# The output stores issued from GpSimd, one transfer of 122 rows in place of 112 + 10 from SP

## Chip, cores, metric

One core of a Trainium2 chip. The metric is the device time of one execution in microseconds (us), on this one core. A time is the median of all runs of a kernel in its call. A run over 1.5% above the fastest of its kernel counts as slow, and ratios use the fast runs alone. "One look" is a single run, whose state is unknown. The profiled execution's span is a little shorter than its time (229.1 us in an execution timed at 230.8).

## The reference

x has shape (8, 3264, 192). A causal convolution over the sequence, seven taps, softmaxed per head, gives a new x. Its first 64 Fourier modes are mixed by complex matrices w_r and w_i, and the result is added back:

```python
X = np.fft.rfft(x, axis=1)                    # x: output of the 7-tap convolution
Yr = einsum(Xr, w_r) - einsum(Xi, w_i)        # modes 0..63
Yi = einsum(Xr, w_i) + einsum(Xi, w_r)
y = np.fft.irfft(Y, n=S, axis=1)
u = x + y
return u + np.maximum(u @ w_ch, 0.0)          # (8, 3264, 192), float32: 20.05 MB
```

What matters here is the output: 8 * 3264 = 26112 rows of 192 floats, 768 bytes each.

## The kernel before

The sequence is cut into 27 windows of 122 rows (the last has 92). A window lies on 122 partitions, so that six rows of history fit beside it in the 128. The loads, which also cast to bf16, go from GpSimd (POOL), all but one small one. The last stage makes two windows of two batches at a time, adds them on VectorE (DVE) into a tile t of four windows, and stores:

```python
p3 = ctx.enter_context(tc.tile_pool(name="p3", bufs=4, side="right"))     # the t tiles
...
def store(q, w0, nw, t):                    # nw = 4 windows, 2 at the end of a pair of batches
    for i in range(2):                      # the two batches of a tile
        dst = out[2 * q + i, WIN * w0:WIN * (w0 + nw), :].rearrange("(k p) e -> p k e", p=WIN)
        for r0, r1 in ((0, 112), (112, WIN)):
            nc.sync.dma_start(out=dst[r0:r1], in_=t[r0:r1, 0:nw, D * i:D * i + D])
...
def finish(item):
    ...
    group_y(combos, zp, t, 2 * k)           # two matmuls, then the add on DVE that writes t (L425)
    if k + 1 == len(work[n]):
        if w0 == NWIN - 1:                  # twice: the 92-row windows of four batches
            dst = out[2 * q:2 * q + 4, WIN * w0:S, :].rearrange("b p e -> p b e")
            nc.sync.dma_start(out=dst, in_=t[0:LASTVALID, 0:2, :].rearrange("p k (b e) -> p (k b) e", b=2))
        else:
            store(q, w0, 2 * len(work[n]), t)
```

There are 56 calls of the inner loop over batches (48 with four windows, 8 with two), so 112 transfers, and two transfers of 92 rows.

Of the kernel before, what the change touches and what calls it, by code (L numbers as in the profile page):

```python
# [18 lines left out]
def kernel(  # L19
# [9 lines left out]
    nc = tc.nc  # L29
    B, S, D = x.shape  # L30
# [6 lines left out]
    WIN = 122  # L37
# [122 lines left out]
    for half in range(2):  # L160
        hs = slice(4 * half, 4 * half + 4)
        for k in range(KK):
            nc.vector.copy_predicated(  # L163
                out=cband[:, hs, :],
# [178 lines left out]
    for g in range(NG4):  # L343
# [20 lines left out]
        for t in range(2):  # L364
            nc.tensor.transpose(et[:, t, :], ymix[:, 64 * t:64 * t + P], ident[:])
        nc.vector.tensor_copy(out=yeT[:, :, 4 * g:4 * g + 4, :],
                              in_=et[:, :, :].rearrange("p t (q k) -> p t q k", q=4)[:, :, :, 0:16])
# [59 lines left out]
    def store(q, w0, nw, t):  # L427
        for i in range(2):
            dst = out[2 * q + i, WIN * w0:WIN * (w0 + nw), :].rearrange("(k p) e -> p k e", p=WIN)
            for r0, r1 in ((0, 112), (112, WIN)):  # L430
                nc.sync.dma_start(out=dst[r0:r1], in_=t[r0:r1, 0:nw, D * i:D * i + D])  # L431

    work = []
    for q in range(B // 2):
# [8 lines left out]
    def finish(item):  # L443
        (n, k, combos), zp = item
        if k == 0:
            tcur[n] = p3.tile([P, 4, 2 * D], F32, tag="t", name="t")
        t = tcur[n]
        group_y(combos, zp, t, 2 * k)
        if k + 1 == len(work[n]):
            q, w0 = work[n][0][0]  # L450
            if w0 == NWIN - 1:
                dst = out[2 * q:2 * q + 4, WIN * w0:S, :].rearrange("b p e -> p b e")
                nc.sync.dma_start(out=dst,
                                  in_=t[0:LASTVALID, 0:2, :].rearrange("p k (b e) -> p (k b) e", b=2))
            else:
                store(q, w0, 2 * len(work[n]), t)
# [47 lines left out]
```

## Time and profile before

| | before |
|---|---|
| time, median | 229.21 us |
| store stage | from about 138 us to the end |
| stores at the 16 DMA engines | busy for 0.92 of their time (the DMA share), about 250 GB/s |
| DVE waiting for a store to free a t buffer | 7.1 us, 8 times |

The kernel has stages with different limits. Only the last one has stores, so it is read by itself: the views restricted to a window, not the averages over the span. The prediction below shows its lines.

### The profile page before, as it was taken

How to read it: one execution, taken by the hardware profiler on the slowest of the kernel's cores; microseconds unless marked ns; L12 is line 12 of the kernel's file. 1: busy time of each engine (PE TensorE's matmuls, PEld its weight loads, DVE VectorE, ACT ScalarE, POOL GpSimd, SP SyncE). 2: the span in 40 equal slices, each digit the busy share in tenths (PEclk: the TensorE clock that was granted, in tenths of full speed). 3: DMA queues.
4: the chain of work that ended last, by engine and by line, in shares of the span. 5: the costliest groups of instructions: out<-in, count | busy, mean ns of one | idle time of the engine just before them, and what ended most of it. 6: DMA issues, size and time to landing. Idle time of an engine off the chain costs nothing.

```text
span 229.1 us, 4342 instructions
## 1 busy us (share of the span) xinstructions
PE 167.1 (73%) x1699; PEld 131.8 (58%) x1699; DVE 116.4 (51%) x211; ACT 101.4 (44%) x132; POOL 70.6 (31%) x121
## 2 busy tenths in 40 slices
PE   0037349989988786768869679999899899989300
PEld 0014248777877564547647458778677677767200
DVE  7897001111111577776654615677676566666510
ACT  2017978778687010100431126566556456546200
POOL 8996343443290457574856000000000000000000
PEclk9999999999999689997995979999999999999965
DMA  2999999999998389999999401899899789988992
GB/s 28 180 177 192 192 192 192 192 192 193 184 140 142 54 129 141 156 163 140 145 183 159 83 1 38 232 245 253 217 269 254 214 207 263 249 250 241 263 263 61
DMA packets 65340, 40.50 MB, mean 177 GB/s; under 512 B 31016, under 2 KB 65320, under 8 KB 65320
## 3 DMA queue, kind: packets, MB, share of 16 engines
q0 software_dynamic: 37600, 20.14, 67.4%
q1 hardware_dynamic: 27720, 20.09, 31.8%
q8 instruction: 13, 0.21, 0.4%
q14 instruction: 7, 0.06, 0.1%
HBM read 40.31 MB, written 20.05 MB: 263 GB/s over the span
## 4 chain that ended last, share of the span: by engine, by line
DMA 33%; PE 31%; DVE 14%; POOL 8%; issue 3%; ACT 3%; SPq 3%; DVEq 0%; POOLq 0%; ACTq 0%
DMA x_all<-in_x_dram 16%; DMA out_dram<-t 8%; DVE cT L273 6%; PE tp L271 6%; DMA wt<-in_moe_w_i_dram 6%; DVE t L425 5%; PE zp L400 5%; PE zp L407 5%; PE zp L405 5%; POOL x_all L63 5%; PE zp L414 4%; DMA win<-in_moe_w_ch_dram 4%; SPq L431 3%; ACT x_all L233 2%; PE yp L349 2%
## 5 line engine op out<-in xcount | busy, mean ns | idle before, releaser
L425 DVE TENSOR_TENSOR t<-zp,x_all 122x768 f32<-122x768 f32 (+1 forms) x54 | 51.3, 957 | 32.3 <-PE zp L414 21.7
L409 ACT ACTIVATE zp<-zp 128x768 f32<-128x768 f32 x54 | 42.9, 795 | 31.4 <-PE zp L407 31.4
L233 ACT CAST x_all<-cp 122x960 bf16<-122x960 f32 (+2 forms) x48 | 39.5, 884 | 22.5 <-PE cp L227 22.3
L405 PE MATMUL zp<-win,cT 128*128 128x192 bf16 x216 | 45.2, 249 | 0.0
L227 PE MATMUL cp<-x_all,cband 128*128 128x240 bf16 (+2 forms) x192 | 27.7, 286 | 19.7 <-DVE cband L163 15.2
L400 PE MATMUL zp<-zwi,gst 128*128 128x384 bf16 x108 | 35.9, 332 | 5.4 <-DVE t L425 4.0
L273 DVE COPY cT<-tp 128x854 bf16<-128x854 bf16 (+2 forms) x48 | 26.9, 590 | 18.3 <-PE tp L271 17.8
L227 PEld LDWEIGHTS <-cband 128*128 128x128 bf16 x192 | 19.4, 108 | 25.2 <-DVE cband L163 15.6
L63 POOL DMA_DIRECT2D x_all<-in_x_dram x24 | 23.8, 1001 | 15.9 <-DMA x_all<-in_x_dram 15.9
L271 PE MATMUL tp<-ident,tl 122*128 122x122 bf16 x112 | 23.2, 243 | 7.0 <-DVE tl L240 5.4
L211 POOL DMA_DIRECT2D wt<-in_moe_w_r_dram x32 | 19.3, 602 | 28.3 <-PE yp L349 21.7
L271 PE MATMUL tp<-ident,x_all 122*128 122x122 bf16 x216 | 26.4, 242 | 2.1 <-DVE cT L273 1.9
L284 PE MATMUL xp<-x_all,fst 122*128 122x192 bf16 (+1 forms) x216 | 22.3, 252 | 7.4 <-ACT fst L178 6.2
L405 PEld LDWEIGHTS <-cT 128*128 128x128 bf16 x216 | 21.4, 99 | 10.5 <-issue 7.7
L414 PE MATMUL zp<-zwi,gst 128*128 128x384 bf16 x108 | 26.2, 326 | 0.2 <-ACT zp L409 0.2
L407 PEld LDWEIGHTS <-cT 128*128 128x128 bf16 x216 | 21.4, 99 | 7.4 <-issue 0.5
L357 ACT CAST ymix<-yp 128x192 bf16<-128x192 f32 x16 | 5.1, 319 | 44.2 <-PE yp L349 44.2
L284 PEld LDWEIGHTS <-fst 122*128 122x128 bf16 (+1 forms) x216 | 18.4, 100 | 8.8 <-ACT fst L178 6.6
L407 PE MATMUL zp<-win,cT 128*128 128x192 bf16 x112 | 23.3, 248 | 0.0
L271 PEld LDWEIGHTS <-x_all 122*128 122x128 bf16 x216 | 18.9, 110 | 5.7 <-issue 4.8
L407 PE MATMUL zp<-wB,cT 128*128 128x192 bf16 x104 | 21.9, 251 | 0.0
L288 DVE CAST xs<-xp 128x192 bf16<-128x192 f32 x8 | 2.9, 358 | 34.3 <-PE xp L284 34.3
(76 smaller groups left out, 158.9 us busy)
## 6 DMA issues: line engine op xcount, KB each, us to landing
out_dram<-t SPq DMA_DIRECT2D x48, 336.0 KB
wt<-in_moe_w_r_dram POOLq DMA_DIRECT2D x32, 144.0 KB, 5.1
wt<-in_moe_w_i_dram POOLq DMA_DIRECT2D x32, 144.0 KB, 5.1
x_all<-in_x_dram POOLq DMA_DIRECT2D x8, 432.0 KB, 16.1
x_all<-in_x_dram POOLq DMA_DIRECT2D x9, 384.0 KB, 17.7
x_all<-in_x_dram POOLq DMA_DIRECT2D x7, 480.0 KB, 18.4
out_dram<-t SPq DMA_DIRECT2D x48, 30.0 KB
out_dram<-t SPq DMA_DIRECT2D x8, 168.0 KB
```

The source lines that it names most:

```text
L63: nc.gpsimd.dma_start(out=x_all[:, b, c0:c0 + n, :], in_=src)
L227: nc.tensor.matmul(cp[:, j, 0:GRP * n].rearrange("p (w e) -> p w e", w=n), cband[:, h, :], x_all[:, b, w0:w0 + n, GRP * h:GRP * h + GRP], ...
L233: nc.scalar.copy(out=dst, in_=srcv)
L271: nc.tensor.transpose(tp[:, WIN * k:WIN * k + WIN], slot_lhsT(b, u, tl, a + k), ident[0:WIN, 0:WIN])
L273: nc.vector.tensor_copy(out=cT[:, b, WIN * a:WIN * (a + cnt)], in_=tp[:, 0:WIN * cnt])
L284: nc.tensor.matmul(xp[:, 0:D], fst[0:k, c, :], x_all[0:k, b, c, :], start=(c == 0), stop=(c == NWIN - 1))
L400: nc.tensor.matmul(zp[:, k, 0:2 * D], gst[:, WIN * w:WIN * w + P], zwi[:, 2 * q:2 * q + 2, 0, :], start=True, stop=False, skip_group_check ...
L405: nc.tensor.matmul(o, cT[:, b, WIN * sa:WIN * sa + P], win0[:, 0:D], start=False, stop=False, skip_group_check=True)
L407: nc.tensor.matmul(o, cT[:, b, WIN * sb:WIN * sb + P], wBs[par], start=False, stop=(i == 1), skip_group_check=True)
L409: nc.scalar.activation(out=zp[:, :, 0:2 * D], in_=zp[:, :, 0:2 * D], func=ACT.Relu)
L414: nc.tensor.matmul(zp[:, k, 0:2 * D], gst[:, WIN * w:WIN * w + P], zwi[:, 2 * q:2 * q + 2, 1, :], start=False, stop=True, skip_group_check ...
L425: nc.vector.tensor_tensor(out=tv, in0=yv, in1=xv, op=ALU.add)
```

## The change

The intent is to take the issue of the stores off SP, to halve their number, and to give the queue of GpSimd, idle by then, something to do.

```diff
     def store(q, w0, nw, t):
         for i in range(2):
             dst = out[2 * q + i, WIN * w0:WIN * (w0 + nw), :].rearrange("(k p) e -> p k e", p=WIN)
-            for r0, r1 in ((0, 112), (112, WIN)):
-                nc.sync.dma_start(out=dst[r0:r1], in_=t[r0:r1, 0:nw, D * i:D * i + D])
+            nc.gpsimd.dma_start(out=dst, in_=t[0:WIN, 0:nw, D * i:D * i + D])
```

The two 92-row transfers stay on SP.

## The prediction

> **What bounds the kernel now.** I read the page first, its 40 slices of busy time, to find the stages:
>
> ```profile
> PE   0037349989988786768869679999899899989300
> DVE  7897001111111577776654615677676566666510
> POOL 8996343443290457574856000000000000000000
> DMA  2999999999998389999999401899899789988992
> GB/s 28 180 177 192 192 192 192 192 192 193 184 140 142 54 129 141 156 163 140 145 183 159 83 1 38 232 245 253 217 269 254 214 207 263 249 250 241 263 263 61
> q1 hardware_dynamic: 27720, 20.09, 31.8%
> ```
>
> A slice is 5.73 us. From slice 24 (about 138 us) on the kernel only stores, PE is near full, and POOL, whose queue carried all loads, is empty. The 20.05 MB output leaves here at about 250 GB/s, so the changed transfers are all in this last stage. Next, the table of stretches cuts it finer (columns after the stretch: its length, then PE, weight loads, DVE, ACT, POOL, the clock, the DMA share, GB/s):
>
> ```profile
> 150.00:160.00 10.00, 10.00 (x94) 8.00 (x93) 7.20 (x9) 5.95 (x8) 0.00 (x0) 1.00 0.92 250
> 180.00:190.00 10.00, 9.26 (x83) 7.24 (x81) 6.20 (x8) 5.35 (x7) 0.00 (x0) 1.00 0.78 205
> 210.00:220.00 10.00, 4.04 (x34) 2.71 (x31) 5.13 (x6) 2.38 (x3) 0.00 (x0) 0.95 0.92 257
> 220.00:229.00 9.00, 0.00 (x0) 0.00 (x0) 0.00 (x0) 0.00 (x0) 0.00 (x0) 0.50 0.47 135
> ```
>
> The reader is to see that the DMA engines stay at 0.92 while PE has already gone quiet, and that nothing but DMA runs in the last 9 us. Then the waits of the stretch from 131 us, and the chain of work that ended last, near its end:
>
> ```profile
> DVE t L425 <- PE zp L414: 21.7, 38, 5.7
> DVE t L425 <- DMA out_dram<-t: 7.1, 8, 1.8
> ```
> ```profile
> 207.66 0.33 PE zp L414 x2
> ...
> 210.72 0.97 DVE t L425
> 211.71 0.96 SPq L431
> 212.71 0.46 SPq L431
> 213.22 4.16 DMA out_dram<-t
> 217.60 0.95 DVE t L425
> ```
>
> DVE's adds into t wait 8 times, 7.1 us in all, for a store to give a t buffer back, and the chain runs through such stores: the stage is bound by the stores, with PE close behind. PE's own pace is 1.31 us per pair of windows (such pairs of L414 rows follow each other at 165.07, 166.38 and 167.69 in the chain), so 54 pairs need 70.7 us; from the first zp at 134.1 to PE's end at 214.3 it took 80.2. Last, the timeline of the SP queue:
>
> ```profile
> 213.22 9.18 SPq L431 DMA_DIRECT2D out_dram<-t  x14
> 222.50 0.26 SPq L453 DMA_DIRECT2D out_dram<-t  x1
> ```
>
> The final t is ready at 218.55, but its store (92 rows, L453) is not issued before 222.50, as SP still works through earlier issues. Then it moves alone; the span ends at 229.1.
>
> **How the stores are spread now.** Queue 1 counts 27720 packets. 8*3264 = 26112 are pieces of 768 bytes of the output, 128 are rows of wraw, and 1480 remain. If 112 rows post a count on 16 engines, 10 rows on 10, 92 rows on 4 and wraw on 16, that is 56*(16+10) + 2*4 + 16 = 1480, exactly. So in a pair of transfers ten engines carry 4*(7+1) = 32 pieces and six 28: mean 30.5, or 0.953 of the most loaded, which is the 0.92 to 0.95 that the share shows when full. The time of a piece is 0.318*16*229.1/27720 = 42 ns per packet, 44 ns when the small ones (about 9 ns each in the packet records) are taken out. The four engines that also carry L453 hold 26*8*8 + 2*92 = 1848 pieces, so 1848*44 ns = 81.3 us, of the 85 us between the first issue at 141.4 plus 1.2 and the end. In the final L453 alone the packet records show one piece per 33 ns per engine.
>
> **What the Trainium skill says.** (1) "DMA: Bandwidth & Descriptors", section "Why a DMA increments its semaphore by 16 and not by 1": the number of engines is the largest up to 16 that divides the slowest dimension. That makes 112 rows 16, 92 rows 4, 122 rows only 2; the packet count above agrees for SP. It adds that transfers issued from GpSimd get, for "some direct copies", all 16 engines with the row count over 16 rounded up per engine. The trace before can't confirm this: its GpSimd transfers have 128, 112, 96, 64, 10 or 2 rows. (2) Same page, "Issuing engines are not separate DMA queues": another issuer saves issue time only. The trace agrees that issue is worth something at the end (3.95 us between 218.55 and 222.50). (3) Same page, "Why small descriptors are slow (HBM only)": bytes/32 beats plus about 3 cycles, so 27 cycles for 768 bytes; at the page's 850 MHz an estimated 31.8 ns. The 33 ns of the lone L453 agrees; the 44 ns of the bulk is a third above it, a backlog that appears only when many engines write. (4) Same page, "Latency and other measured facts": first byte 1 us after a GpSimd issue, 0.6 us after a hardware one. The trace has GpSimd's first small loads landing in 2.0 to 2.5 us.
>
> **The change, part by part.**
> Removed: 112 issues on SP (median 0.53 us, 60 us of SP's time). Only the two of L453 remain there (the instruction order shows it), so the last one can go right after its add: at most 3.95 us gained at the end.
> Added: 56 issues on POOL. From the page's rows,
>
> ```profile
> L63 POOL DMA_DIRECT2D x_all<-in_x_dram x24 | 23.8, 1001 | 15.9 <-DMA x_all<-in_x_dram 15.9
> L211 POOL DMA_DIRECT2D wt<-in_moe_w_i_dram x32 | 19.6, 612 | 1.9 <-DMA x_all<-in_x_dram 1.4 <-issue 0.5
> ```
>
> 612 ns for 128 pieces and about 1000 for some 1150, hence about 0.38 ns a piece: 612 + 360*0.38 = 0.75 us for the 488 pieces of a store, 48*0.75 + 8*0.66 = 41 us in all, on an engine with no work from 138 us on. Against the SP path a store starts about 0.5 us later, its twin 0.75 us after it.
> Waits: the instruction order has each store wait for the one 8 transfers earlier on its kind of queue. On SP that was two t tiles (4 transfers each); from GpSimd it is four tiles, just as many as there are t buffers. So dips in feeding, like 0.78 at 180 to 190 us, should shrink.
> Moved bytes: the same. With 8 rows an engine (rounded up from 122/16) fifteen engines carry 32 pieces and one 8: the most loaded engine has 32 as before. No gain from balance.
> Sum, if all 16 engines are used: at 44 ns a piece the four worst engines need 81.3 us from about 143.1, so 224.4, plus 1.2 us to the end as now, 225.6. At 40 ns a tile takes 64*40 = 2.56 us, below PE's 2.62: PE binds. The first L414 at 138.65 plus 53*1.31 plus three more zwi groups of about 0.6 gives 210, plus 1 for the add, 0.6 for issue, 1 for the start, 92*40 ns = 3.7 of L453, which shares its four engines with the last backlog (2 more), plus 1.2: 219.5. I expect between these, near 222, as queue 0 kept a steady 192 GB/s into bf16 from twice as many source bytes for 40 us, so that descriptors written by GpSimd do not by themselves slow an engine at 768 bytes.
>
> **Rivals.**
> A: 122 rows get only 2 engines each. A store takes 244 pieces, at 33 to 44 ns 8.1 to 10.7 us. A tile's buffer is held 2.3 (fill) + 1.5 (two issues) + 1 + about 9.4 = 14.2 us; four buffers give a tile per 3.55 us against 2.62 of PE. 24 full tiles and 4 halves at some 2.2 make 94 us, then a tail of 10: about 246. For it: the divisor rule, which SP obeys to the packet, and the before kernel's own split of GpSimd loads into 112 + 10 and 96 + 2. Against it: the page's exception. I give it 0.3.
> B: all engines, but stores are slower by this path, say 50 ns a piece (descriptors are fetched from SBUF, and rows are now 8*768 bytes apart between engines): 143.1 + 1848*0.050 + 1.2 = 236.7. Nothing in the trace speaks for it, as no store goes this way yet; 0.15.
> C: the bulk is limited by what HBM takes, 265 GB/s whoever issues. Then only feeding and the tail improve: 224 to 228, about the same. That the lone L453 ran at 33 ns and the bulk at 44 speaks for it; 0.2.
> The main case, 219 to 224, keeps 0.35.
>
> **Range and chances.** Faster by over 2% means under 224.6: the main case and a part of C, 0.43. Within 2%: the rest of C and edges of B, 0.19. Slower: A and most of B, 0.38. Point 222, range 214 to 250, which is wide because A is a different mode and not an error bar.
>
> **What would show it.** Right: POOL issues of 0.75 us; queue 0 with 25376 more data packets and 56*16 counts; DMA share 0.9 or more without the dip at 180; DVE's waits for stores below 7.1 us; L453 issued within 1 us of the last add; a mean piece of 44 ns or less. Wrong: stores landing after 10 us with a DMA share well under 0.9 and PE waiting (A), or mean pieces of 50 ns with full engines (B).

## The result and the profile after

The changed kernel takes 450.27 us (448.78 and 451.76) beside 229.21 us: a ratio of 1.96, 95% interval 1.92 to 2.01. Ratios here are the mean time of one kernel's fast runs over that of the other's of the same rounds, so not quite the ratio of the medians quoted.

The page of the changed kernel, its slices (11.25 us each here), its packet count and queue 0:

```profile
PE   0449988667669431643083404307432436030000
POOL 9744452666605342647064406515264644356230
DMA  8999996999920334244423432441434344333541
GB/s 100 184 192 192 192 159 99 150 156 152 190 41 8 70 69 78 53 79 68 73 45 74 77 69 38 91 84 33 79 73 91 59 73 84 62 64 75 84 75 27
DMA packets 73580, 41.21 MB, mean 92 GB/s; under 512 B 60360, under 2 KB 69304, under 8 KB 73560
q0 software_dynamic: 72672, 40.35, 59.3%
```

Up to about 138 us the stages are those of before. Then, for 310 us, the stores run at about 70 GB/s, with a DMA share of 0.4, PE mostly idle, and POOL half busy. Before it was 0.9 and 250 GB/s. The costliest groups and the issues:

```profile
L430 POOL DMA_DIRECT2D out_dram<-t x56 | 134.0, 2394 | 181.1 <-issue 141.9
L425 DVE TENSOR_TENSOR t<-zp,x_all 122x768 f32<-122x768 f32 (+1 forms) x54 | 50.4, 955 | 234.5 <-DMA out_dram<-t 209.8
out_dram<-t POOLq DMA_DIRECT2D x48, 366.0 KB, 21.9
out_dram<-t POOLq DMA_DIRECT2D x8, 183.0 KB, 19.8
```

(After the bar: busy us, mean ns of one; then the idle time before them and what ended most of it. In the issue lines: KB each, median us from issue to landing.) An issue takes 2.39 us in the mean, not the 0.75 that I had worked out, a store lands after 21.9 us, and DVE waits 209.8 us for stores where it waited 7.1. GpSimd itself sits idle 141.9 us before its stores for nothing the profile can name. Its timeline at the start of the stage:

```profile
140.63 9.89 POOL L430 DMA_DIRECT2D out_dram<-t  x4 [18.34 <-DVE t L425]
159.86 2.45 POOL L430 DMA_DIRECT2D out_dram<-t  x1 [9.33 <-issue]
164.40 2.45 POOL L430 DMA_DIRECT2D out_dram<-t  x1 [2.08 <-issue]
168.97 2.45 POOL L430 DMA_DIRECT2D out_dram<-t  x1 [2.12 <-issue]
```

Four stores go out one behind the other, and then each waits for something that the profile doesn't name. I take it for room in GpSimd's queue; runs 11 and 12 test that.

**The packets say what a store has become.** A piece is one contiguous run of a transfer, here a row of 768 bytes; a packet is what the profiler keeps one record for. From SP each piece is a packet of its own, from GpSimd up to six pieces are one. The bytes moved grew from 40.50 to 41.21 MB though the output is the same, and the packets below 512 bytes from 31016 to 60360. In the packet records queue 0 now has 4160 packets of 4608 bytes (six pieces of 768), 96 of 3072 and 16 of 1536, and with each of these exactly seven tiny ones: 29120 of 24 bytes, 672 of 16, 112 of 8, that is six, four or two pieces of 4 bytes. The large ones fit two engines: 244 pieces each are 40 packets of six and one of four, so 48 * 2 * 40 + 8 * 2 * 20 = 4160 and 48 * 2 = 96. Seven tiny packets for each real one are 14 engines for 2. The whole count closes: 4272 real packets, eight times that with the tiny ones, and 56 * 16 semaphore counts make 35072, and 72672 - 37600 = 35072. So do the bytes: 25376 pieces * 7 * 4 bytes = 0.71 MB.

So a store of 122 rows has its real pieces on 2 engines, and the other 14 each get as many empty pieces of 4 bytes. Its 488 pieces become 16 * 244 = 3904 entries to write, and the issue is three times as long. It doesn't grow in proportion to the entries: the stores of two windows, with half of them, still take 2.01 us, and in run 3 below a transfer of 116 rows and four windows, with 16 * 116 entries, takes 1.50. Even the kernel before had this in small: 1540 counts on queue 0 for 95 transfers are 95 * 16 + 20, and the 20 are 6 empty pieces of its 10-row load and 14 of its 2-row load. I had left those 20 unexplained.

### The profile page after: what moved, and what is told of

It is laid out like the page before. It is cut to its first block, busy times and chain, and to the rows that moved or that the text cites. A ratio compares the mean times of both kernels' runs of the same rounds, so it can differ in the third digit from the quotient of the medians.

```text
span 450.0 us, 4258 instructions
## 1 busy us (share of the span) xinstructions
PE 195.5 (43%) x1699; PEld 145.6 (32%) x1699; DVE 115.2 (26%) x211; ACT 101.3 (23%) x132; POOL 204.5 (45%) x177
## 2 busy tenths in 40 slices
DMA packets 73580, 41.21 MB, mean 92 GB/s; under 512 B 60360, under 2 KB 69304, under 8 KB 73560
## 3 DMA queue, kind: packets, MB, share of 16 engines
q0 software_dynamic: 72672, 40.35, 59.3%
## 4 chain that ended last, share of the span: by engine, by line
issue 28%; POOL 20%; DMA 19%; PE 15%; DVE 10%; ACT 4%; POOLq 1%; DVEq 0%; ACTq 0%
POOL out_dram L430 18%; DMA out_dram<-t 17%; DVE cT L273 4%; PE xp L284 3%; ACT x_all L233 3%; PE cp L227 3%; PE tp L271 2%; DVE cband L163 2%; DVE t L425 2%; PE zp L400 1%; DMA wt<-in_moe_w_i_dram 1%; PE zp L405 1%; PE zp L407 1%; PE zp L414 1%; DMA wt<-in_moe_w_r_dram 1%
## 5 line engine op out<-in xcount | busy, mean ns | idle before, releaser
L430 POOL DMA_DIRECT2D out_dram<-t x56 | 134.0, 2394 | 181.1 <-issue 141.9
L400 PE MATMUL zp<-zwi,gst 128*128 128x384 bf16 x108 | 45.2, 418 | 158.6 <-DVE t L425 157.2
L425 DVE TENSOR_TENSOR t<-zp,x_all 122x768 f32<-122x768 f32 (+1 forms) x54 | 50.4, 955 | 234.5 <-DMA out_dram<-t 209.8
L405 PEld LDWEIGHTS <-cT 128*128 128x128 bf16 x216 | 25.8, 119 | 169.0 <-issue 166.9
L405 PE MATMUL zp<-win,cT 128*128 128x192 bf16 x216 | 58.4, 302 | 0.0
L414 PE MATMUL zp<-zwi,gst 128*128 128x384 bf16 x108 | 34.4, 410 | 0.2 <-ACT zp L409 0.2
L407 PEld LDWEIGHTS <-cT 128*128 128x128 bf16 x216 | 26.4, 122 | 13.3 <-issue 9.0
L407 PE MATMUL zp<-win,cT 128*128 128x192 bf16 x112 | 30.0, 300 | 0.0
L407 PE MATMUL zp<-wB,cT 128*128 128x192 bf16 x104 | 28.1, 302 | 0.0
L271 PE MATMUL tp<-ident,x_all 122*128 122x122 bf16 x216 | 23.1, 220 | 3.0 <-DVE cT L273 2.9
L271 PE MATMUL tp<-ident,tl 122*128 122x122 bf16 x112 | 19.8, 223 | 7.1 <-DVE tl L240 4.9
L211 POOL DMA_DIRECT2D wt<-in_moe_w_i_dram x32 | 19.6, 613 | 1.9 <-DMA x_all<-in_x_dram 1.4
L271 PEld LDWEIGHTS <-x_all 122*128 122x128 bf16 x216 | 16.7, 99 | 5.6 <-issue 4.2
## 6 DMA issues: line engine op xcount, KB each, us to landing
out_dram<-t POOLq DMA_DIRECT2D x48, 366.0 KB, 21.9
```

Of the source, the lines that this page charges most:

```text
L211: nc.gpsimd.dma_start(out=wt[64 * half:64 * half + 64, :, :, :], in_=src[MG * g:MG * g + MG, :, :].rearrange("m (p j) e -> p m j e", j=3))
L271: nc.tensor.transpose(tp[:, WIN * k:WIN * k + WIN], slot_lhsT(b, u, tl, a + k), ident[0:WIN, 0:WIN])
L400: nc.tensor.matmul(zp[:, k, 0:2 * D], gst[:, WIN * w:WIN * w + P], zwi[:, 2 * q:2 * q + 2, 0, :], start=True, stop=False, skip_group_check ...
L405: nc.tensor.matmul(o, cT[:, b, WIN * sa:WIN * sa + P], win0[:, 0:D], start=False, stop=False, skip_group_check=True)
L407: nc.tensor.matmul(o, cT[:, b, WIN * sb:WIN * sb + P], wBs[par], start=False, stop=(i == 1), skip_group_check=True)
L425: nc.vector.tensor_tensor(out=tv, in0=yv, in1=xv, op=ALU.add)
```

## The experiments

Two theories. **R**, the row count: 122 has no larger divisor up to 16 than 2; a transfer with 2 engines is slow from any queue, and from GpSimd it also fills the queue with empty pieces. **I**, the issuer: stores from GpSimd are slow as such. The first four runs tell them apart, beside the kernel before (229.22 us).

**1. GpSimd, cut into 112 and 10 rows again** (3 rounds)

```diff
-            nc.gpsimd.dma_start(out=dst, in_=t[0:WIN, 0:nw, D * i:D * i + D])
+            for r0, r1 in ((0, 112), (112, WIN)):
+                nc.gpsimd.dma_start(out=dst[r0:r1], in_=t[r0:r1, 0:nw, D * i:D * i + D])
```

> The stores stay on GpSimd, but each is cut into 112 and 10 rows again. Theory R (row count: 122 rows have 2 as their largest divisor up to 16, so a store's real pieces lie on 2 engines, and the other 14 get as many empty 4-byte pieces, which fill the descriptor rings and lengthen the issue): the mean issue falls from 2.45 us to about 0.7, the 24-byte packets vanish, GpSimd hardly waits for room, and the time comes back to 222 to 236 us (112 issues of 0.68 us are 76 us of an 80 us stage, so a little slower than before is possible). Theory I (stores written by GpSimd are slow as such): still over 300 us, landing over 10 us.

Measured: 246.21 us, ratio 1.087 (1.069 to 1.105). Landing 5.0 us. The group of its issues:

```profile
L431 POOL DMA_DIRECT2D out_dram<-t x112 | 71.1, 642 | 41.9 <-DVE t L425 34.4 <-DMA out_dram<-t 4.8 <-issue 2.1
```

The issue is 642 ns, the 24-byte packets are gone, and of 141.9 us of waiting for room 2.1 are left. So of the 221 us of slowdown about 204 come from the row count and 17 from the issuer (20 by the fast runs alone). The record calls the verdict on run 1 unclear: only two of the seven runs of the kernel before were fast in this call. It is slower than R's range of 222 to 236, so something else is left over for theory I; runs 5 and 6 take it up.

**2. SP, one transfer of 122 rows** (one look)

```diff
-            nc.gpsimd.dma_start(out=dst, in_=t[0:WIN, 0:nw, D * i:D * i + D])
+            nc.sync.dma_start(out=dst, in_=t[0:WIN, 0:nw, D * i:D * i + D])
```

> The stores go back to SP, but as one transfer of 122 rows. Theory R: 2 engines again, and if the hardware queue always takes the same ones, each has 25376/2 = 12688 pieces at 33 to 36 ns, 419 to 457 us for the stage: 560 to 610 us in all, with no empty pieces (queue 1 has 2*56 + 2*4 + 16 = 136 counts beside 26112 + 128). If the engines rotate: 240 to 300. Theory I: the issuer is what mattered, so 225 to 235 us.

Measured: 572.85 us, one run; no GpSimd store in it at all.

```profile
GB/s 118 191 192 192 154 98 151 150 179 1 43 47 47 48 47 47 47 47 48 47 47 47 47 47 56 48 47 47 47 47 48 47 47 47 47 47 47 47 47 49
q1 hardware_dynamic: 26376, 20.08, 10.4%
```

26376 packets are 26112 + 128 + 136, as expected to the packet, and the rate is flat at 47 GB/s, two engines with 768 bytes per 33 ns each. A piece lasts 36.2 ns in the mean. SP stays on the same two engines for the whole stage; GpSimd's 70 GB/s is more than two engines gave here, so its stores must take different engines in turn. Theory I alone falls: with the row count of the change, the old issuer is even slower.

**3. GpSimd, 116 and 6 rows** (one look; 116 has the divisor 4)

```diff
-            for r0, r1 in ((0, 112), (112, WIN)):
+            for r0, r1 in ((0, 116), (116, WIN)):
```

> GpSimd, 116 rows (largest divisor up to 16: 4) and 6 rows. Theory R: in the large transfer four engines carry 116 pieces each in place of two with 244, and twelve get 116 empty ones; with the small one a store takes 120 places in each engine's ring in place of 244, the large issue is about 0.6 + 16*116*0.5 ns = 1.5 us, and the stage shrinks to roughly half: 290 to 330 us. Theory I: within 5% of the 450 us, or longer because of twice the transfers.

Measured: 345.53 us. The packet records have 3936 packets of 4608 bytes and 11808 of 24 bytes, three to one: 12 empty engines to 4. The direction and the kind are R's, and the total is 15 us above the range I gave.

**4. GpSimd, 122 rows, two windows at a time** (one look)

```diff
-            nc.gpsimd.dma_start(out=dst, in_=t[0:WIN, 0:nw, D * i:D * i + D])
+            for k in range(0, nw, 2):
+                nc.gpsimd.dma_start(out=dst[:, k:k + 2], in_=t[0:WIN, k:k + 2, D * i:D * i + D])
```

> GpSimd, 122 rows, each 4-window store cut into two of 2 windows: the same pieces, the same empty ones, twice the transfers at half the size. If room in the rings is what limits (4 large stores, nearly 1000 pieces per engine, fit before GpSimd waits), 8 small ones fit, so 16 engines instead of 8 work at a time: the stage shrinks clearly, 300 to 380 us. If the number of transfers in flight or the writing of descriptors is the limit (2.45 us per 3904), the total stays at 430 to 470 us.

Measured: 444.45 us, so within the range for a limit by the number of transfers or by writing entries. GpSimd no longer waits for room (2.4 us) but needs 2.01 us for each half, so 104 issues take 209 of 282 us, and it waits 65.1 us for earlier stores. The wait for room was replaced by two other limits. By itself this run does not say how much the room had cost.

**5. Run 1 with the 92-row stores cut into 80 and 12 rows** (3 rounds). Run 1's profile has a hole right after the first 92-row store, which SP issues at 180.79 us:

```profile
170.00:180.00 10.00, 7.92 (x72) 6.11 (x70) 5.01 (x6) 5.18 (x7) 8.52 (x14) 1.00 0.85 225
180.00:190.00 10.00, 2.50 (x12) 1.66 (x12) 0.81 (x2) 0.80 (x1) 3.39 (x6) 0.55 0.57 152
190.00:200.00 10.00, 8.63 (x60) 6.42 (x60) 5.61 (x7) 3.76 (x5) 5.09 (x8) 0.77 0.42 118
```

(The table of stretches of run 1, columns as in the prediction.)

```diff
-                nc.sync.dma_start(out=dst,
-                                  in_=t[0:LASTVALID, 0:2, :].rearrange("p k (b e) -> p (k b) e", b=2))
+                for r0, r1 in ((0, 80), (80, LASTVALID)):
+                    nc.sync.dma_start(out=dst[r0:r1],
+                                      in_=t[r0:r1, 0:2, :].rearrange("p k (b e) -> p (k b) e", b=2))
```

> GpSimd stores of 112 and 10 rows as in the run before (246 us), and the two 92-row stores, which stay on SP, cut into 80 and 12 rows (16 and 12 engines in place of 4). Theory L (what is left of the slowdown comes largely from the 92-row store: on its 4 engines each of its 92 pieces of 768 bytes takes turns with a GpSimd packet of six pieces, so it lasts far over 4 us, keeps its buffer, and stalls the stage, 9 us at 181 us and again at the end): the dip at 180 to 200 us goes, 230 to 237 us. Theory P (GpSimd's 112 issues of 0.64 us, 72 us of the stage, and only two tiles in flight are what is left): 242 to 247 us, with the dip only smaller.

Measured: 236.59 us, ratio 1.031 (1.024 to 1.039): theory L's range, barely. The hole is shallower, and DVE waits 10.2 us for stores in the stage, at most 4.3 at a time, against 20.8 and 9.2 in run 1:

```profile
180.00:190.00 10.00, 6.71 (x37) 4.43 (x36) 3.40 (x4) 2.75 (x4) 4.84 (x8) 0.68 0.75 207
190.00:200.00 10.00, 10.00 (x91) 8.02 (x90) 6.71 (x7) 5.76 (x8) 7.58 (x12) 0.98 0.58 155
```

My picture of it was too crude: the packets of the first 92-row store in run 1 span 6.2 us, so it does not wait for a full GpSimd packet with each of its pieces, which would have been some 25 us. The cut took the ratio from 1.087 to 1.031 here, on two chips, and to 0.977 in run 6, where all stores go from SP. So the 92-row store probably costs more beside GpSimd's packets; by which mechanism is not shown. (In the two profiles 3.3 us of the 9.8 between runs 1 and 5 lie before the first store, which the cut does not touch.)

**6. The kernel before with that same cut, all on SP** (5 rounds). The edit is run 5's, on the kernel before.

> The kernel before with its two 92-row stores cut into 80 and 12 rows, all on SP. The four most loaded engines go from 1848 pieces to 1712, 6 us less at 44 ns, and the last transfer ends about 2.5 us sooner; if the stage is bound by its most loaded engines, as I argued: 222 to 226 us. If another wait sets it: 226.5 to 229.

Measured: 225.13 us beside 230.42, ratio 0.977 (0.969 to 0.985). This is the fastest version and beats both kernels, though whether by 2% is unclear, as the interval has 0.98 in it. The profiles don't settle where the gain arises: of the 7.1 us between them (229.1 and 222.0) 4.0 lie before the first store (141.4 and 137.4 us), which the edit does not touch, 0.5 between the first and the last issue of a store, and 2.6 after it. With the same cuts, GpSimd's 236.59 against SP's 225.13 leaves about 11 us for the issuer (13 by the fast runs). What these consist of is not shown.

**7. As run 6, with the 10-row transfers from GpSimd** (5 rounds)

```diff
-            for r0, r1 in ((0, 112), (112, WIN)):
-                nc.sync.dma_start(out=dst[r0:r1], in_=t[r0:r1, 0:nw, D * i:D * i + D])
+            nc.sync.dma_start(out=dst[0:112], in_=t[0:112, 0:nw, D * i:D * i + D])
+            nc.gpsimd.dma_start(out=dst[112:WIN], in_=t[112:WIN, 0:nw, D * i:D * i + D])
```

> As the kernel of the line above, but the 10-row transfers go from GpSimd (56 issues of about 0.6 us) and the 112-row ones from SP. Twice as many transfers may be in flight on each queue (four tiles in place of two) and SP issues half as many. If feeding the engines still costs: 217 to 222 us. If the engines' own pace is all there is: the same as the kernel above within 1%; and slower if the mixing of packet sizes at the engines hurts as it did the 92-row store.

Measured: 230.17 us median over all six runs, 225.14 to 233.3; ratio of the two fast ones 0.986 (0.975 to 0.996). No gain over run 6: halving SP's issues and allowing more in flight bought nothing. The intervals of runs 6 and 7 overlap, so a loss is not shown either.

**8. GpSimd, 120 and 2 rows** (one look; the edit is run 1's with 120). 120 has the divisor 15.

> GpSimd, 120 and 2 rows; the 92-row stores as before on SP. 120 has the divisor 15: fifteen engines with 8 rows each, 32 pieces, and one with 32 empty ones. That is just how rounding 122/16 up would have spread a whole store. Theory R: within 4% of the 246 us of the 112 and 10 rows. If large transfers with rows not a multiple of 16 are slow as such on this queue: over 290 us.

Measured: 251.18 us, 2% over run 1. It was run on another chip. Fifteen engines with 8 rows each are just what rounding 122/16 up would have given to a whole store, so the prediction's main case had an outcome near 250 even with its own spread.

The last four runs ask why two engines per store cost so much more than the 246 us of rival A. They were run at other times. First, how many stores are in flight.

**9 and 10. The changed kernel with one and with two t buffers** (one look each)

```diff
-p3 = ctx.enter_context(tc.tile_pool(name="p3", bufs=4, side="right"))
+p3 = ctx.enter_context(tc.tile_pool(name="p3", bufs=1, side="right"))      # run 10: bufs=2
```

> The changed kernel with one t buffer in place of four: at most two stores can be in flight. Theory F (each store takes its time, and how many fit in flight sets the rate: 21.9 us to landing with four in flight is one per 5.3 us): two in flight give one tile per about 2.3 + 2.5 + 2.5 + 13 to 22 us, 20 to 29 us for 28 tiles, so 700 to 950 us. Theory S (the stores share something that passes about 70 GB/s, and a store only waits its turn): the time to landing falls to about half, near 11 us, and the total stays under 520 us.

> The changed kernel with two t buffers: at most four stores in flight, as many as GpSimd got into the rings with four buffers. If room in the rings (about 4 stores of 244 places on every engine) is the limit with four buffers, two are nearly as good: 450 to 475 us, with the waits of GpSimd for room nearly gone. If four buffers had really carried more stores at once: over 500 us.

Measured: 719.11 us with one buffer, 503.85 with two, 450.27 with four. Median landings are 16.1, 20.2 and 21.9 us for the large stores; the lines of runs 9 and 10:

```profile
out_dram<-t POOLq DMA_DIRECT2D x48, 366.0 KB, 16.1
out_dram<-t POOLq DMA_DIRECT2D x48, 366.0 KB, 20.2
```

Run 9 is in theory F's range: a store takes about 16 us even when only its twin is in flight, and the number in flight sets the rate. Some sharing is there too, as the landing grows by a third from two to four. Run 10 missed the 450 to 475 of the theory of room, and lies in the range of its rival, over 500, that four buffers had carried more stores at once. GpSimd waited 232.9 us for t in it, so it could not keep four in flight: the two stores of a tile must both land, and the tile must be filled again, before the next goes out. That reading is argued, not tried, and run 10 does not settle the room in the queue.

**11 and 12. Stores with nothing to wait for** (one look each). On run 2's kernel GpSimd also stores zeros into parts of batches 4 to 7, which the proper stores overwrite much later; the result is right.

```diff
+    junk = junkp.tile([P, 4, D], F32, tag="junk")
+    nc.gpsimd.memset(junk[:], 0.0)
+    for b in range(4, 8):
+        for j in range(6):
+            nc.gpsimd.dma_start(                     # run 11: ROWS = 122, run 12: ROWS = 112
+                out=out[b, WIN * 4 * j:WIN * 4 * (j + 1), :].rearrange("(k p) e -> p k e", p=WIN)[0:ROWS],
+                in_=junk[0:ROWS])
```

> All stores from SP as 122 rows (573 us, each piece 36 ns, two engines), and at the start of the store stage GpSimd also writes zeros with 24 stores of 122 rows into parts of the output that the proper stores overwrite much later. Theory D (the empty pieces of a 122-row GpSimd store slow down real pieces on other engines and queues): while they run, the mean of a 768-byte piece of SP rises from 36 ns to 45 or more, the median too. If they do no harm, the median stays 36 and the mean rises only by the eighth of stores whose own real pieces are on SP's two engines, to about 50 at most with a long tail. The 24 stores themselves wait for no t buffer: if the 5.3 us per store of the changed kernel is the queue's own pace and not the buffers', they take about 127 us. Total 573 to 700 us.

> The control for the line above: the same 24 stores of zeros with 112 rows, all 16 engines and no empty pieces. They should be over within 24*1.5 to 24*2.5, 36 to 60 us (344 KB each at 150 to 230 GB/s), issue 0.7 us each; SP's pieces then share their two engines with packets of six pieces: the median stays 36 ns, the mean rises to 40 to 60 in that time. Total within 30 us of 573.

Measured: 668.33 us and 596.09 us. GpSimd's timeline in run 11, then in run 12:

```profile
130.91 9.89 POOL L462 DMA_DIRECT2D out_dram<-junk  x4 [0.30 <-POOL junk L459]
149.66 2.45 POOL L462 DMA_DIRECT2D out_dram<-junk  x1 [8.86 <-issue]
153.71 2.45 POOL L462 DMA_DIRECT2D out_dram<-junk  x1 [1.60 <-issue]
```
```profile
133.58 7.05 POOL L462 DMA_DIRECT2D out_dram<-junk  x10 [0.30 <-POOL junk L459]
141.16 0.71 POOL L462 DMA_DIRECT2D out_dram<-junk  x1 [0.53 <-DMA out_dram<-junk]
```

With 122 rows GpSimd stops after four issues although it has no t to wait for and no earlier transfer to watch before its ninth; with 112 it issues ten in a row. In run 12 a store lands after 10.6 us and one goes out every 1.5 us, so some seven of about the same size are in flight: neither the number of transfers nor their bytes stops GpSimd at four. What fits is a room of about four times 244 entries per engine. In the packet records the 24 stores of run 11 take 145.0 us, 6.0 each; in run 12 35.1 us, 1.5 each. The changed kernel's pace of 5.4 us per store is the queue's own, and its t buffers only pass it on.

Do the empty pieces slow real ones? While run 11's stores ran, an SP piece lasted 60.9 ns in the mean against 36.2 otherwise, but its median stayed 36, and in the control of run 12 the mean was 45.7. By the test I had set, a risen median, harm is not shown; the mean is above the 50 that I allowed for none. But that test sees only how long a piece lasts once it has started, and the totals say more. Run 12 took 23 us more than run 2, and run 11 took 95 us more, although GpSimd gave an engine about as many real pieces in both: 24 * 448/16 = 672 and 24 * 488/16 = 732, if its stores are spread evenly, which the records do not tell. About 70 us are left over. Only run 11 has the empty pieces, 21 * 244 on an engine, which makes an estimate of 14 ns for each, or 82 ns for a packet of six whose record shows 13. The packet records of two other runs point the same way:

- The 92-row stores from SP take 17.3 and 11.3 us from first to last packet in the changed kernel, 6.2 and 5.7 in run 1.
- In run 9 a packet of six real pieces lasts 219 ns in the mean where no 24-byte packet starts within 0.5 us of its start (690 packets), and 340 where 100 or more do (1439 packets).

With this estimate eight stores bring an engine one real share, 41 packets at their median of 191 ns, and seven empty ones, 41 packets at 82 ns each: 31 us, or 3.9 of the 5.4 us per store. This was read after the fact. No run took away the empty pieces alone, so their harm is likely and not shown.

## Why the prediction was wrong

- **The bound, and where the change acts: right.** The stage is bound by stores. Run 6 fits: with 136 fewer pieces on the four most loaded engines it was about 5 us faster, where 136 * 44 ns gives 6; its profile does not confirm that the gain arises there.
- **The step that failed: how 122 rows are spread.** I gave 0.7 to all 16 engines, on the Trainium skill's remark about "some direct copies" ("DMA: Bandwidth & Descriptors", the section cited in the prediction), and wrote that the trace could not confirm it. The measured spread is 2 engines, from GpSimd as from SP. The line "Sum, if all 16 engines are used" describes a kernel that did not run.
- **Rival A had the cause and a size of 246 us in place of 450.** Three terms were too small. The issue: 0.75 us assumed, 2.45 measured, with the empty entries of 14 engines among what it writes. The stores in flight: four tiles, eight stores assumed; the room ended at four stores. The time of a store: 8.1 to 10.7 us of moving assumed at 33 to 44 ns a piece; a six-piece packet lasted 315 ns in the mean, so 52 ns a piece, and a store landed after 21.9 us, 16 with only two in flight. The median packet lasted 191 ns, 32 a piece, as assumed: it is the slow part of the packets that A left out, and the empty pieces are the likely cause. Four in flight over 21.9 us is one store per 5.5 us; measured between first and last issue it is (435.4 - 140.6)/55 = 5.4, and A had 3.55/2 = 1.8.
- **Rival B, 50 ns a piece by this path: not so where 16 engines work.** In run 1 six pieces took 275 ns, 46 each, beside 44 from SP.
- **The issue cost for well spread transfers: right,** 0.64 to 0.71 us in runs 1 and 12. **The issuer's own cost: missed.** I expected a gain from it; it cost 17 to 20 us, of which 11 to 13 are left with the cut of the 92-row stores on both sides. So the main case would have missed with its own spread too: run 8, spread as it assumed, took 251.18 us.
- **The earlier last store: right and without value.** SP issues its last store at 418.9 us, but GpSimd's last one goes at 435.4.
- **The signs that I named for A were the ones that came:** landing over 10 us, a DMA share well below 0.9, PE waiting.

## What to carry to other kernels

Before merging transfers, or moving them to another queue, look at the row count: its largest divisor up to 16 was the number of engines that worked in every store here (122 gave 2, 116 gave 4, 120 gave 15, 112 gave 16). 112 + 10 beats 122 by a factor of 1.8 from GpSimd (246 us against 450) and 2.5 from SP (229 against 573). From GpSimd a badly divisible count also costs issue time and room, as the unused engines get an empty entry for each real one, and it probably holds up what else these engines carry. Check it without a timing: count the packets of a queue and see whether they close.

## What the Trainium skill lacked or had wrong

- "DMA: Bandwidth & Descriptors", section "Why a DMA increments its semaphore by 16 and not by 1": its exception, 16 engines with the rows over 16 rounded up for some direct copies from GpSimd, did not hold for any of the stores here. 122 rows gave 2 engines and 116 gave 4 by the packet counts; the page does not say which copies it means.
- The same section has no word on empty pieces: on GpSimd's queue every engine without data got as many 4-byte pieces as the others have real ones (29904 tiny packets to 4272 real ones), and the issue grew from 0.71 us (112 rows) to 2.45 us (122 rows).
- The room of GpSimd's descriptor rings, which take the entries that it writes, stands in "SBUF — State Buffer", section "SBUF size: 192, 224, or 256?", as 16 KiB of each partition. No page says how many stores or entries per engine that is. Here it ended at four stores of 244 entries per engine, after which the issuer waited 8.9 to 9.3 us.
- "DMA: Bandwidth & Descriptors", section "Issuing engines are not separate DMA queues", says that issuing from several engines at once only saves the time of issuing. It puts no figure on the choice of one issuer or another; the page only calls the path from SP generally faster. Here the same cuts took 236.6 us from GpSimd and 225.1 us from SP.
